# Signs written into half-words, weight bounds from Gram products, and a new order of work in a packed-attention and SoLU kernel

## The chip, the core and the metric

The kernel runs on one core of one Trainium2 chip. What counts is the device time of one execution, in microseconds; lower is better. Several executions were timed, and the median is given. The profile is of one execution more, and has its own time.

## What is computed

Eight batches of attention feed a two-layer network. First 32 learned rows `p` per head attend over 576 keys, and the result is used as both keys and values for the 576 queries. The output, 4608 tokens of 512 numbers, goes through a 512x1024 matrix, a softmax-weighted gate, a normalisation of each row and a 1024x512 matrix:

```python
p_packed = sm_attn(p, k, v)                    # 8 batches, 8 heads, 32x64
x = sm_attn(q, p_packed, p_packed)             # 576x64 for each head -> 4608 x 512
h = x @ w_in
e = np.exp(h - h.max(-1)); sm = e / (e.sum(-1) + 1e-09)
solu = h * sm
ln = (solu - mean) / np.sqrt(var + 1e-06) * g_ln
out = ln @ w_out                               # 4608 x 512
```

The two weight matrices arrive as float64. The kernel reads such a number as two 32-bit words and builds a float32 from them.

## The kernel before

**Stages.** All work is cut into named steps. `ORDER` (line 26 on) is a long string of step names; `perform` issues the steps in exactly that order, and `issue` chains all instructions of one engine in it. So each engine works through its own list, and a step that has to wait holds up whatever stands behind it on its engine. A letter behind a name picks the engine (`a` ScalarE, `v` VectorE, `p` GpSimd), a number the PSUM bank. Every load is issued from SyncE's queue (SP), in order too.

**Weights** (steps with `/w`, chunks 0 to 3 of `w_in`, 4 to 7 of `w_out`, 1 MB each). `lw`/`lW` loads a chunk into a buffer that later holds something else (`W_HOME`). `wa` (`exponents`) scales the upper words, `wl` (`last_bits`) shifts the lower words, `wm` (`magnitude`) joins the two, `wp` (`column_sums`) adds up the sizes on TensorE, and `ws` (`signed`) puts the sign in. `wb` (`bound_in`) and `pw` (`scale_out`) make powers of two from the sums. With these, `zw`, `zy` split `w_in`, and `ch`, `cl` split `w_out`, into pairs of f16 parts.

**Attention** (steps with `/b` for batch b). Keys, values and queries are loaded by `lk`, `lv`, `lq`. `s10`, `s11` are the first scores, `mx` their maxima (tile `nmx`), `ex` the exponentials, `tp` and `tc` their transposes, `av`, `pp`, `pt`, `pc` the packed rows, `un` the scale of the batch. `sx`, `sb`, `sm`, `su`, `se`, `ss`, `sn`, `at` are the second softmax; `ah`, `al` its f16 pair (tiles `a2h`, `a2l`). `z`, `zh`, `zl` multiply the packed rows by `w_in`, as an f16 pair.

**Token tiles** (steps with `-i`, 36 tiles of 128 rows). `m1` (line 642, 12 products of 512 columns, about 2.6 us) needs `a2` and `z` of its batch. Then come `nm`, `nb`, `bd`, `ex`, `u`, `mu`, `yd`, `yh`, `yl` on the other engines, `tr` (a DMA transpose), `m2a` and `m2b` (line 726, 24 products), `ev` and `st`, which stores the tile.

The scales that a step puts in place of a plain copy go through one helper, so line 139 or 141 in a profile stands for many steps, and the tile name tells which.

## Time and profile before

| | us |
|---|---|
| median of three runs | 392.41 (392.32 to 393.96) |
| time of the profiled execution | 392.76 |
| its span | 391.0 |
| TensorE busy in the span | 363.8 (93%) |
| VectorE busy | 297.0 (76%) |
| ScalarE busy | 229.3 (59%) |
| GpSimd busy | 193.7 (50%) |

The span is what the profile covers, from the first instruction to the end of the last store; the execution's own time is 1.76 us longer. Busy shares are means over the whole span. The first quarter and the rest of this kernel differ, so they are read by stretches below.

### The profile page before, as it was taken

Reading aid. Unit: us, or ns where it says so; the run is one execution under the profiler, and the core shown is the slowest. Engines: PE = TensorE matmul, PEld = TensorE weight load, DVE = VectorE, ACT = ScalarE, POOL = GpSimd, SP = SyncE. Lnnn points to the kernel's source line nnn. Section 1 sums busy time; section 2 is a strip of 40 time slices with the busy share of each in tenths; the row PEclk is TensorE's granted clock in tenths of the full one; section 3 lists DMA queues with packets and bytes.
Section 4 is the critical chain, followed back from the end, with each engine's and each line's share of the span. In section 5 each row is a group of like instructions: output and inputs, shape, how many; then the busy total and the mean of one; then the engine's idle time right before and its main releaser. Section 6 shows DMA issues by size and latency. Waiting matters only on the chain.

```text
span 391.0 us, 7708 instructions
## 1 busy us (share of the span) xinstructions
PE 363.8 (93%) x3056; PEld 168.3 (43%) x3056; DVE 297.0 (76%) x433; ACT 229.3 (59%) x367; POOL 193.7 (50%) x287
## 2 busy tenths in 40 slices
PE   5683879999999999999999999999999999999996
...
PEclk9575789999999999999999999999999999999999
...
GB/s 265 426 417 375 407 407 67 228 175 91 55 271 206 274 266 56 82 230 54 240 146 40 179 145 77 140 147 126 80 82 82 108 107 55 80 109 113 157 163 81
DMA packets 87957, 66.57 MB, mean 170 GB/s; under 512 B 76400, under 2 KB 76528, under 8 KB 86384
## 3 DMA queue, kind: packets, MB, share of 16 engines
...
## 4 chain that ended last, share of the span: by engine, by line
PE 67%; DVE 20%; DMA 4%; issue 3%; ACT 2%; POOL 1%; SPq 1%; DVEq 0%; ACTq 0%; POOLq 0%
PE pa L726 31%; PE ps L642 18%; PE ps L726 8%; DMA kT<-in_k_dram 3%; DVE u L671 3%; PE ps L534 2%; PE ps L476 2%; DVE nmx L400 2%; PE pa L442 2%; DVE zl L552 1%; DMA qT<-in_q_dram 1%; DVE ssum L411 1%; PE ps L396 1%; DVE wcl L296 1%; DVE e L202 1%
## 5 line engine op out<-in xcount | busy, mean ns | idle before, releaser
L726 PE MATMUL pa<-wch,yT 128*128 128x512 f16 x448 | 139.0, 380 | 0.3 <-DMA yT<-yhl 0.2
L726 PEld LDWEIGHTS <-yT 128*128 128x128 f16 x864 | 82.4, 98 | 105.8 <-issue 9.7
L726 PE MATMUL pa<-wcl,yT 128*128 128x512 f16 x224 | 84.9, 379 | 0.0
L671 DVE SCALAR_TENSOR_TENSOR u<-e,s_row,ps 128x1024 f32<-128x1024 f32 x36 | 45.9, 1275 | 19.0 <-ACT e L666 10.0
L648 DVE TENSOR_REDUCE nm<-ps 128x1 f32<-128x1024 f32 x36 | 43.7, 1218 | 19.2 <-PE ps L642 19.1
L642 PE MATMUL ps<-zh,a2h 128*128 128x512 f16 (+1 forms) x160 | 54.9, 381 | 0.7 <-DVE zl L552 0.4
L642 PE MATMUL ps<-zh,a2l 128*128 128x512 f16 (+1 forms) x160 | 54.6, 379 | 0.0
L642 PE MATMUL ps<-zl,a2h 128*128 128x512 f16 (+1 forms) x160 | 54.6, 379 | 0.0
L698 POOL TENSOR_TENSOR yhl<-u,yhl 128x1024 f16<-128x1024 f32 x16 | 35.3, 2206 | 37.8 <-ACT yhl L692 19.8
L666 ACT ACTIVATE e<-ps,bias,unit 128x1024 f32<-128x1024 f32 x36 | 43.3, 1203 | 9.1 <-DVE bias L141 8.4
L642 PEld LDWEIGHTS <-a2h 128*128 128x128 f16 (+1 forms) x320 | 27.7, 100 | 35.3 <-issue 5.2
L726 PE MATMUL ps<-wch,yT 128*128 128x512 f16 x128 | 39.9, 379 | 0.0
L659 POOL TENSOR_SCALAR bound<-nm,unit 128x1 f32<-128x1 f32 x20 | 10.9, 546 | 45.6 <-DVE nm L648 45.6
L682 ACT ACTIVATE u<-u,negmu 128x1024 f32<-128x1024 f32 x21 | 24.1, 1147 | 14.3 <-DVE negmu L141 9.5
L139 ACT ACTIVATE o_sb<-pa,c_row 128x512 f32<-128x512 f32 x16 | 11.0, 685 | 28.5 <-PE pa L726 16.1
L719 POOL TENSOR_TENSOR c_row<-c_row,neg_half 128x1 f32<-128x1 f32 x36 | 24.3, 674 | 3.0
L726 PE MATMUL ps<-wcl,yT 128*128 128x512 f16 x64 | 24.3, 379 | 0.0
L139 ACT ACTIVATE bias<-nm,unit 128x1 f32<-128x1 f32 x21 | 6.2, 295 | 30.0 <-DVE nm L648 29.8
L407 ACT ACTIVATE e<-ps,nmx 128x576 f32<-128x576 f32 x16 | 11.8, 736 | 19.6 <-DVE nmx L400 19.6
L700 DVE SCALAR_TENSOR_TENSOR yhl<-u,negmu,yhl 128x1024 f16<-128x1024 f32 x15 | 20.4, 1359 | 2.6 <-ACT yhl L694 2.5
L708 ACT ACTIVATE e<-u 128x1024 f32<-128x1024 f32 x21 | 22.1, 1051 | 0.1
L642 PEld LDWEIGHTS <-a2l 128*128 128x128 f16 (+1 forms) x160 | 14.3, 100 | 16.8 <-issue 0.2
...
## 6 DMA issues: line engine op xcount, KB each, us to landing
kT<-in_k_dram SPq DMA_DIRECT2D x16, 576.0 KB, 6.9
v<-in_v_dram SPq DMA_DIRECT2D x8, 1152.0 KB, 8.3
qT<-in_q_dram SPq DMA_DIRECT2D x16, 576.0 KB, 6.0
...
zl<-in_moe_w_in_dram SPq DMA_DIRECT2D x2, 1024.0 KB, 9.0
zh<-in_moe_w_in_dram SPq DMA_DIRECT2D x2, 1024.0 KB, 8.2
kT<-in_moe_w_out_dram SPq DMA_DIRECT2D x1, 1024.0 KB, 14.4
qT<-in_moe_w_out_dram SPq DMA_DIRECT2D x1, 1024.0 KB, 16.7
```

What stands on the lines that cost most here:

```text
L139: nc.scalar.activation(out, in_, AF.Copy, scale=scale)
L407: nc.scalar.activation(dst, src, AF.Exp, bias=st['nmx', r], accum_out=st['es'][:, r:r + 1])
L642: nc.tensor.matmul(h[rows, 512 * n:512 * n + 512], lhsT=lhsT, rhs=z[:, r, 512 * n:512 * n + 512], start=t == 0, stop=t == end)
L648: nc.vector.tensor_reduce(out=nm, in_=st['h'], axis=AX.X, op=ALU.max, negate=True)
L666: nc.scalar.activation(st['e'], st['h'], AF.Exp, bias=st['bias'], scale=st['unit'][:, 1:2], accum_out=st['se'])
L671: nc.vector.scalar_tensor_tensor(out=st['u'], in0=st['e'], scalar=st['s_row'], in1=st['h'], op0=ALU.mult, op1=ALU.mult, accum_out=st['su'])
L682: nc.scalar.activation(st['u'], st['u'], AF.Identity, bias=st['negmu'])
L698: engines[on(f'yl-{i}', 'v')].tensor_tensor(out=st['y'][:, 1], in0=st['u'], in1=st['y'][:, 0], op=ALU.subtract)
L700: nc.vector.scalar_tensor_tensor(out=st['y'][:, 1], in0=st['u'], scalar=st['negmu'], in1=st['y'][:, 0], op0=ALU.add, op1=ALU.subtract)
L708: nc.scalar.activation(st['e'], st['u'], AF.Square, bias=0.0 if centred() else st['negmu'], accum_out=st['sq'])
L719: nc.gpsimd.tensor_tensor(out=c_row, in0=c_row, in1=neg_half, op=ALU.pow)
L726: nc.tensor.matmul(st['po'], lhsT=st['yT'][:, a, c], rhs=w[:, c], start=c == 0 and t == 0, stop=c == NFC - 1 and t == 2)
```

## The change

**Sign.** A new step `wg` (`sign_bit`) writes each weight times 2^-60 as f16 into the upper half-words of the tile that holds the last bits. The product is too small for f16, so a zero with the weight's sign is left, and that is the sign bit of the word. `wl` now writes only the lower half-words of that tile. One step `wm` (`combined`) then joins exponent, last bits and sign on VectorE, where two did it; `ws` is gone. `wg` runs on ScalarE for chunks 0, 1 and 6 and on VectorE for 2, 3, 4, 5 and 7.

**Bounds.** `wp` (`squares`) now multiplies each 128-column piece of a chunk by itself on TensorE, eight products of 128 columns for a chunk where there were two of 512. `wb0`/`pw0` take the largest entry of each row on VectorE, `wb1`/`pw1` spread these over all partitions with a product, and `wb`/`pw` take the maximum again and an approximate root (`root`: a shift and an addition). The gain's bound comes from the sum of its squares (`gx`), and the GpSimd step `gm` is gone.

**Unread products.** `unread` issues four products of 512 columns whose result nobody reads. `ORDER` places four such steps: `hw5` and `hw11` among the loads of the weights, `hw13` and `hw2` behind the last `m2b` of the program.

**Places.** The whole string `ORDER` is new, with other engines for many steps. `unit` tiles have five buffers instead of four.

```diff
-lw1/w lw0/w wa1/w:a wl1/w:a wm1/w wa0/w:v wl0/w:a lp0/w wm0/w wp0/w:6 wp1/w lg/w ws1/w gx/w ws0/w lw2/w wa2/w:v pC0/w:p
...
+lW0/w wa4/w:p wl4/w wg4/w:v wm4/w lW1/w wa5/w:p wl5/w wp4/w:6 wg5/w:v wm5/w lW2/w wa6/w:a wl6/w wg6/w:a wm6/w wp5/w
...
     def last_bits(n):
-        last_of[n] = mlp.tile([P, DF], I32, name='u', bufs=2)
+        word = word_of(n)
         words = words_of(w_raw[n])[0]
...
-            nc.scalar.activation(last_of[n], words.bitcast(U32), AF.Copy, scale=LAST)
-
-    def magnitude(n):
-
-        bits = bits_of[n] = bits_of[n].bitcast(I32)
-        nc.vector.scalar_tensor_tensor(out=bits, in0=bits, scalar=3, in1=last_of[n], op0=ALU.logical_shift_left, op1=ALU.bitwise_or)
...
-    def column_sums(n):
-        m = n // 4
-        if n % 4 == 0:
-            sums[m] = one()
-        for i in range(2):
-            nc.tensor.matmul(sums[m], lhsT=g_abs[0][:, 2 * (n - 4) + i] if m else ones_b, rhs=upper(bits_of[n], i), start=n % 4 + i == 0, stop=n % 4 == 3 and i == 1)
-
-    def signed(n):
+            nc.scalar.activation(word.bitcast(U16)[:, 0::2], words.bitcast(U32), AF.Copy, scale=LAST)
+
+    def sign_bit(n):
+
+        scaled(on(f'wg{n}/w', 'a'), word_of(n).bitcast(F16)[:, 1::2], words_of(w_raw[n])[1].bitcast(F32), 2.0 ** (-60))
...
+    def combined(n):
+
...
-        nc.vector.scalar_tensor_tensor(out=dst.bitcast(I32), in0=words_of(w_raw[n])[1], scalar=-2147483648, in1=bits_of[n], op0=ALU.bitwise_and, op1=ALU.bitwise_or)
+        value[n] = dst
+        nc.vector.scalar_tensor_tensor(out=dst.bitcast(I32), in0=bits_of[n].bitcast(I32), scalar=3, in1=last_of[n], op0=ALU.logical_shift_left, op1=ALU.bitwise_or)
+
+    def squares(n):
+        m = n // 4
+        if n % 4 == 0:
+            sums[m] = one()
+        for i in range(NFC):
+            part = value[n].bitcast(BF16)[:, 2 * P * i + 1:2 * P * (i + 1):2]
+            nc.tensor.matmul(sums[m][:, :P], lhsT=part, rhs=part, start=n % 4 + i == 0, stop=n % 4 == 3 and i == NFC - 1)
+
+    def peaks(m):
+        peak_of[m] = small.tile([P, 1], F32, name=f'w_peak{m}')
+        nc.vector.tensor_reduce(out=peak_of[m], in_=sums[m][:, :P], axis=AX.X, op=ALU.max)
+
+    def spread(m):
+        nc.tensor.matmul(sums[m][:, P:2 * P], lhsT=peak_of[m].broadcast_to([P, P]), rhs=ident, start=True, stop=True)
...
+    def unread(dep):
+        spot = one()
+        for i in range(4):
+            ins = nc.tensor.matmul(spot, lhsT=ones_b, rhs=ones_b.unsqueeze(1).broadcast_to([P, 4, P]), start=True, stop=True)
...
```

**What moves, at three places.** SyncE's queue from its first load on, before (the name ahead of the arrow is the buffer; `in_moe_w_in` and `in_moe_w_out` are the weights, `in_k`, `in_v`, `in_q` the inputs of batch 0):

```order
L174 DMA zl<-in_moe_w_in_dram 128x2048
L174 DMA zh<-in_moe_w_in_dram 128x2048
L157 DMA pT<-in_p_dram 128x256
L164 DMA g_sb<-in_moe_g_ln_dram 128x8
L174 DMA zh<-in_moe_w_in_dram 128x2048
L378 DMA kT<-in_k_dram 128x1152 x2
L174 DMA zl<-in_moe_w_in_dram 128x2048
L382 DMA v<-in_v_dram 128x2304
L378 DMA qT<-in_q_dram 128x1152
L174 DMA kT<-in_moe_w_out_dram 128x2x1024
```

And the same queue from its first load on, after the change:

```order
L175 DMA kT<-in_moe_w_out_dram 128x2x1024
L175 DMA qT<-in_moe_w_out_dram 128x2x1024
L175 DMA v<-in_moe_w_out_dram 128x2x1024
L175 DMA zh<-in_moe_w_out_dram 128x2x1024
L165 DMA g_sb<-in_moe_g_ln_dram 128x8
L175 DMA zl<-in_moe_w_in_dram 128x2048
L175 DMA zh<-in_moe_w_in_dram 128x2048
L158 DMA pT<-in_p_dram 128x256
L410 DMA kT<-in_k_dram 128x1152 x2
L175 DMA zl<-in_moe_w_in_dram 128x2048
L414 DMA v<-in_v_dram 128x2304
L175 DMA zh<-in_moe_w_in_dram 128x2048
```

All four chunks of `w_out` now go ahead of the first keys, which three chunks of `w_in` went ahead of; two of `w_in` still do.

VectorE from the maxima of batch 0's first scores (`nmx`) on, before (`e`, `u` hold a chunk's exponents and last bits):

```order
L400 TENSOR_REDUCE nmx<-ps_76 128x1
L400 TENSOR_REDUCE nmx<-ps_77 128x1
L195 TENSOR_SCALAR u<-zh 128x1024
L202 SCALAR_TENSOR_TENSOR e<-e,u 128x1024
L411 TENSOR_SCALAR ssum<-es 128x2
L413 RECIPROCAL rs<-ssum 128x2
L219 SCALAR_TENSOR_TENSOR w_in_sb<-zh,e 128x1024
L202 SCALAR_TENSOR_TENSOR e<-e,u 128x1024
L219 SCALAR_TENSOR_TENSOR w_in_sb<-zl,e 128x1024
L453 TENSOR_REDUCE peak<-pp 128x1
```

And the same engine from the same two maxima on, after the change:

```order
L432 TENSOR_REDUCE nmx<-ps_76 128x1
L432 TENSOR_REDUCE nmx<-ps_77 128x1
L216 SCALAR_TENSOR_TENSOR w_in_sb<-e,u 128x1024
L327 SCALAR_TENSOR_TENSOR wcl<-yhl,gs,wch 128x512
L327 SCALAR_TENSOR_TENSOR wcl<-yT,gs,wch 128x512
L443 TENSOR_SCALAR ssum<-es 128x2
L445 RECIPROCAL rs<-ssum 128x2
L216 SCALAR_TENSOR_TENSOR w_in_sb<-e,u 128x1024
L327 SCALAR_TENSOR_TENSOR wcl<-yT,gs,wch 128x512
L148 COPY e1T<-ps_76 128x128
L327 SCALAR_TENSOR_TENSOR wcl<-yhl,gs,wch 128x512
```

Where a chunk cost two joins of 1024 columns there is one, and the low parts of `w_out` (`wcl`), which stood behind the start of the token tiles, fill the room.

TensorE up to the first products of token tile 3 (`a2h`, `zh`), before (`kT,pT` are first scores, `e` transposes of exponentials, `v,e1T` weighted values, `qT,ppT` second scores):

```order
L442 MATMUL pa_80<-v,e1T 32x64 x40
L458 MATMUL pa_79<-ident,pp 128x128 x2
L419 MATMUL pa_80<-ident,e_459 128x128 x4
L476 MATMUL ps_76<-qT,ppT 32x288 x8
L476 MATMUL ps_78<-qT,ppT 32x288 x8
L642 LDWEIGHTS a2h_101
L642 MATMUL ps_77<-zh,a2h_101 128x512
```

And the same stretch after the change:

```order
L474 MATMUL pa_79<-v,e1T 32x64 x40
L451 MATMUL pa_80<-ident,e_586 128x128 x4
L490 MATMUL pa_79<-ident,pp 128x128 x2
L451 MATMUL ps_77<-ident,e_586 128x128 x4
L508 MATMUL ps_78<-qT,ppT 32x288 x8
L456 MATMUL pa_80<-ident,e_586 64x64 x4
L508 MATMUL ps_76<-qT,ppT 32x288 x8
L428 MATMUL ps_77<-kT,pT 32x288 x8
L497 LDWEIGHTS ones_b
L497 MATMUL pa_79<-peak,ones_b 128x1
L428 MATMUL ps_78<-kT,pT 32x288 x8
L674 LDWEIGHTS a2h_101
```

The rest of batch 2's transposes, both halves of batch 3's first scores and one product on `peak` now stand ahead of tile 3.

## Rows read from the trace of the kernel before

**Rows 1.** The profile's page: span, engines, and three of its rows of 40 slices.

```profile
span 391.0 us, 7708 instructions
...
PE 363.8 (93%) x3056; PEld 168.3 (43%) x3056; DVE 297.0 (76%) x433; ACT 229.3 (59%) x367; POOL 193.7 (50%) x287
...
PE   5683879999999999999999999999999999999996
...
PEclk9575789999999999999999999999999999999999
...
GB/s 265 426 417 375 407 407 67 228 175 91 55 271 206 274 266 56 82 230 54 240 146 40 179 145 77 140 147 126 80 82 82 108 107 55 80 109 113 157 163 81
```

**Rows 2.** Busy time by stretches: PE, PEld, DVE, ACT, POOL; PEclk, DMA, GB/s.

```profile
55.00:100.00 45.00, 42.38 (x507) 20.47 (x507) 42.37 (x64) 34.48 (x64) 32.54 (x39) 1.00 0.49 153
100.00:380.00 280.00, 279.08 (x2088) 125.69 (x2083) 209.34 (x309) 161.65 (x253) 131.05 (x227) 1.00 0.51 134
```

**Rows 3.** TensorE in order of time: start, us, engine, line, operands, count.

```profile
13.72 2.53 PE L396 MATMUL ps<-kT,pT 64*32 64x288 f32 x32 [0.91 <-DMA kT<-in_k_dram]
...
54.75 0.50 PE L642 MATMUL ps<-zh,a2h 128*128 128x512 f16 x1
...
61.71 0.72 PE L396 MATMUL ps<-kT,pT 64*32 64x288 f32 x16
...
67.37 0.60 PE L419 MATMUL pa<-ident,e 128*128 128x128 f32 x4
...
386.70 0.38 PE L726 MATMUL pa<-wch,yT 128*128 128x512 f16 x1
```

**Rows 4.** The chain that ended last, in order of time, in its first 20 us.

```profile
3.77 11.23 DMA kT<-in_k_dram
```

**Rows 5.** VectorE in order of time, 0 to 55 us.

```profile
8.88 0.69 DVE L141 TENSOR_SCALAR e<-zh 128x1024 f32<-128x1024 f32 x1
9.67 1.23 DVE L202 SCALAR_TENSOR_TENSOR e<-e,u 128x1024 int32<-128x1024 int32 x1
...
17.75 2.13 DVE L202 SCALAR_TENSOR_TENSOR e<-e,u 128x1024 int32<-128x1024 int32 x1
...
25.79 0.15 DVE L242 TENSOR_SCALAR w_pow<-w_pow 128x1 f32<-128x1 f32 x1
...
26.93 0.78 DVE L498 STREAM_TRANSPOSE s<-ps 128x576 f32<-128x576 f32 x1
...
31.83 2.46 DVE L552 SCALAR_TENSOR_TENSOR zl<-ps,unit,zh 128x1024 f16<-128x1024 f32 x2
34.22 0.73 DVE L511 TENSOR_REDUCE sm<-s 128x18 f32<-128x576 f32 x1
...
48.51 1.41 DVE L400 TENSOR_REDUCE nmx<-ps 128x1 f32<-128x576 f32 x2
...
53.70 0.73 DVE L296 SCALAR_TENSOR_TENSOR wcl<-yhl,gs,wch 128x512 f16<-128x512 f32 x1
```

**Rows 6.** DMA issues: KB each, us from issue to landing.

```profile
kT<-in_k_dram SPq DMA_DIRECT2D x16, 576.0 KB, 6.9
v<-in_v_dram SPq DMA_DIRECT2D x8, 1152.0 KB, 8.3
...
zl<-in_moe_w_in_dram SPq DMA_DIRECT2D x2, 1024.0 KB, 9.0
...
pT<-in_p_dram SPq DMA_DIRECT2D x1, 128.0 KB, 8.0
```

**Rows 7.** GpSimd in order of time.

```profile
17.69 2.85 POOL L141 TENSOR_SCALAR e<-zl 128x1024 f32<-128x1024 f32 x1 [3.34 <-DMA zl<-in_moe_w_in_dram]
...
46.23 3.49 POOL L569 TENSOR_TENSOR a2l<-s,a2h 128x576 f16<-128x576 f32 x2 [0.41 <-ACT a2h L145]
```

**Rows 8.** ScalarE in order of time.

```profile
6.60 1.10 ACT L197 ACTIVATE u<-zl 128x1024 int32<-128x1024 uint32 x1
...
46.20 0.68 ACT L145 CAST a2h<-s 128x576 f16<-128x576 f32 x1
```

More of the change, by code (lines that the diff above doesn't have):

```diff
@@ L12 @@
 U32 = mybir.dt.uint32
+U16 = mybir.dt.uint16
 AF = mybir.ActivationFunctionType
@@ new lines @@
+wp6/w hw5/w:7 lW3/w wa7/w:a wl7/w wg7/w:v wm7/w wp7/w lg/w hw11/w:7 pw0/w lw1/w wa1/w:a lw0/w wa0/w:p gx/w pw1/w lp0/w
+pC0/w:a pw/w ch6/w:v lk0/0 lk1/0 wl1/w wg1/w:a s10/0:0 wl0/w s11/0:2 mx0/0 mx1/0 ch4/w:p lw3/w lv/0 wm1/w cl6/w ex0/0
+ex1/0 cl4/w rs/0 tp0/0:7 tp1/0:6 tp2/0:0 wg0/w:a wm0/w ch0/w:p ch5/w:a cl0/w tc0/0:a tc1/0:a tc2/0:v av/0:7 ch7/w:a
+cl7/w wp0/w:6 wa3/w:v wl3/w wg3/w:v wp1/w lw2/w wa2/w:a wl2/w wg2/w:v ch2/w:a wm3/w pp/0:a pt/0:7 lq0/0 pc/0:a lp1/w
+sx0/0:4 cl2/w pe/0 wm2/w wp2/w sb0/0 sm0/0 wp3/w wb0/w pC1/w:a lk0/1 su0/0:p s10/1:2 mx0/1 ex0/1 lk1/1 s11/1:0 mx1/1
@@ L90 @@
+sq-35 m2a-34:6 ca-33 cr-34 m2b-34 ca-28 mu-33:p cr-28 ex-31 u-31 yd-33:a yh-33:a yl-33:p ev-28:v tr-35 m2a-35:7 m2b-35
+mu-31:v yd-31:a tr-33 m2a-33:0 m2b-33 sq-33 ev-34:v yh-31:a yl-31:v st-34 st-28 tr-31 m2a-31:6 ca-31 cr-33 cr-35 ev-35:v
+m2b-31 st-35 ev-33:a st-33 sq-31 cr-31 hw13/w:7 hw2/w:7 ev-31:a zz/7 st-31
 '''
@@ L304, in unit_of @@
     def unit_of(b, total):
-        unit = units[b] = small.tile([P, 6], F32, name='unit', bufs=4)
+        unit = units[b] = small.tile([P, 6], F32, name='unit', bufs=5)
         power_of(unit[:, 5:6], total, unit[:, 4:5])
@@ L357, in issue @@
         fn(*args)
+        made[now[0]] = nc.cur_bb.bb.instructions[-1].name
         for ins in nc.cur_bb.bb.instructions[n:]:
@@ L763, in preparation @@
         at('gx', gain_sizes, after=['lg'])
-        at('gm', gains, after=['gx'])
         for n in range(8):
```

178 lines of the change are left out of this document (95 added, 83 removed).

## The prediction

> **What bounds the kernel now.** I read the page first, then the busy time by stretches, then TensorE and VectorE in order of time. On the page TensorE is busy for 93% of the span, but its slices show two kernels: a start of six slices, some 55 us, with holes and a clock far below full, and a rest that is full [rows 1]. The stretches say it more sharply. From 100 to 380 us TensorE is busy for 279.08 of 280 us at full clock, from 55 to 100 us for 42.38 of 45 us, while VectorE has room in the rest (209 of 280 us) [rows 2]. So the reader can take the kernel as a queue of TensorE work that begins with the first product of token tile 3, at 54.75 us, and ends with the last product at 386.70 + 0.38 = 387.08 us [rows 3]. Between them lie 332.3 us, of which 2.6 + 0.9 = 3.5 us are idle, so 328.8 us of work. Call the beginning F. The time can change by F, by what is done ahead of F, and by those 3.5 us. Joins saved on VectorE are worth nothing by themselves after 100 us.
>
> What sets F? Before it VectorE hardly stops: the chain of its operations runs from the landing of batch 0's keys at 3.77 + 11.23 = 15.0 us [rows 4] to the maxima of batch 2's first scores, whose end is 48.51 + 1.41 = 49.9 us [rows 5], and F follows 4.9 us later. The loads are the other limit: over the first six slices they move 265 to 426 GB/s [rows 1], so bytes in front of the keys are time.
>
> **The change, part by part.**
>
> *Loads.* Before, three weight chunks, a piece of `p` and the keys come to 3 x 1.05 + 0.13 + 2 x 0.59 = 4.46 MB by 15.0 us [rows 4, 6]. A slice is 9.775 us; the slices give 2.59 MB by 9.8 us and 4.81 MB by 15.0 us [rows 1], so 0.35 MB of later loads are then already moved. After it, six chunks go ahead: 7.60 + 0.35 = 7.95 MB. The slices reach 6.75 MB at 19.55 us and go on at 417 GB/s, so the keys land at 22.4 us, 7.4 us later than before. That is a loss, and the VectorE work that filled those 7.4 us must be gone for it to be paid back.
>
> *VectorE.* The `w_out` joins lie ahead of the keys now, where VectorE waits for loads anyway (2 us of each 2.5 us chunk: one join of 1.23, one sign of 0.69 [rows 5]), so I cost them at nothing; the late loads hide them. What is left from the keys to batch 2's maxima, counted from the new order: 4 joins at 1.23 (4.9), 3 scalings or signs at 0.69 (2.1), 6 low parts `wcl` at 0.73 (4.4), 6 maxima at 0.70 (4.2), 3 transposes at 0.78 (2.3), 3 reductions over 576 at 0.73 (2.2), one `zl` at 1.23, and 19 short ones at 0.15 plus some 0.05 between them (3.8) [rows 5]: 25.1 us. Before, this stretch took 34.9 us, with eleven joins in it. A sign written with a step of two half-words stands in no row. Its bounds are 0.69, the scaling of float32 with a step, and 1.23, the join; I take 0.69, being the same kind of operation, and 1.23 would add 1.1 us for the two signs here.
>
> *Slowed operations.* The join at 17.75 took 2.13 us where the one at 9.67 took 1.23 [rows 5]; a GpSimd scaling ran from 17.69 to 20.54 us beside it [rows 7]. Four of those eleven joins were slowed so, by 0.8 to 1.0 us. GpSimd has less to do in the new stretch (one `e` and one `w_hi` scaling less), so I count one slowed operation, 0.9 us; both ends are in the rivals. The Trainium skill, "SBUF — State Buffer", Terms, says that VectorE and GpSimd share a port pair under an exclusive lock held for the whole instruction, and that the loser fully blocks. Here the rows differ from it: the join began 0.06 us after the GpSimd scaling and ended at 19.88 us, 0.66 us ahead of it. By the rows the sum gets 0.9 us; by the rule it would get up to 2.85 us.
>
> *F.* VectorE starts on the list at about 23 us and ends at 23 + 25.1 + 0.9 = 49.0 us. Behind it stand a sum of three operations (1.1), two short ones (0.3), `zl` (1.2) and a transpose (0.8), to 52.4 us [rows 5], then ScalarE's `a2h` at 0.68 [rows 8] and GpSimd's `a2l` at 1.75 [rows 7]: F = 54.9, say 55.0 us. The later keys and the shorter list cancel.
>
> *ScalarE* gains three signs of about 1.10 us [rows 8], with slack: they stand by the loads. *TensorE*: the squares, eight products of 128 columns for two of 512, and the eight spare products of `hw5`, `hw11` lie where it waits for chunks; without that cover the spare ones would cost 3.4 us at half clock. `hw13` and `hw2` stand behind the last product, beside the last store; the end has 391.0 - 387.1 = 3.9 us for that, and they take 8 x 0.21 = 1.7 us.
>
> *Work moved ahead of F.* Both halves of batch 3's first scores (0.65 each: the 0.72 is followed 0.64 us later by the next work), the rest of batch 2's transposes (0.44 + 0.38) and a peak product (0.1): 2.2 us [rows 3]. They are in TensorE's holes there, so they leave the queue for good.
>
> *Idle after F.* Of the 3.5 us, most lies between 55 and 100 us, where VectorE is busy for 42.37 of 45 us [rows 2]. Seven `wcl` stood there before, two do now: 5 x 0.73 = 3.7 us less in front of the maxima and gates that TensorE waits for. Against it, 2.2 us of cover are gone that TensorE had while tile 3 was on its way to `m2a`. The ends are 0 and 3.7; I take 1.5 us.
>
> **The sum.** 55.0 + 328.8 - 2.2 + 1.5 = 383.1 us for the last product, + 3.9 = 387.0 us span against 391.0. The profiled execution took 1.76 us more than its span, so 388.8 against its 392.76; the median lies 0.35 below that execution: **388.4 us** against 392.41. A measurement here can tell about 0.5%, 1.96 us, from no change, so this is faster if it falls under 390.4.
>
> **Rivals.**
>
> 1. *The list runs clean* (faster still). No operation is slowed (0.9 less), and no idle is left after F (1.5 less); the loads keep 426 GB/s, the best slice [rows 1], which brings the keys 0.3 us earlier. 388.4 - 2.7 = 385.7. For it: less GpSimd work. Against: four of eleven were slowed before.
>
> 2. *GpSimd slows as before* (no change). 13 operations of the list are joins, `wcl`, scalings or signs. At four in eleven, 4.7 of them lose 0.9, 4.2 in all: 3.3 more than I count, F = 58.3, and 391.7. The signs at 1.23 alone would give 389.5. For it: `wch` and `w_hi` scalings of GpSimd still lie in the stretch. By the lock as a mechanism, the same 4.7 operations would wait 2.85 each: 13.4 - 0.9 = 12.5 more, and 400.9. The Trainium skill, "SBUF — State Buffer", Terms, is the page for it. The trace speaks against it, as above, so it gets 2 in 100.
>
> 3. *The loads become the bound of F* (slower). Batch 3's keys must now land ahead of tile 3, because its first scores stand there in TensorE's queue. All that is loaded ahead of them and they come to 18.9 MB, 19.25 with what runs ahead; the slices reach 18.47 MB at 48.9 us and 19.25 at 50.8 us [rows 1]. First scores of 1.3 us then end at 52.1, 2.9 us ahead of F. These keys need a buffer that the scores of batch 1 give back. If TensorE comes to those late (they stand behind the squares of the last `w_in` chunk), SP's queue stops, and with it every load behind. From F = 59 on, with the keys landing near 57.7, the gain of 4.0 us is gone; at F = 61.5 it is 394.9. For it: 7 us that the change has already spent. Against it: 17.8 MB of earlier loads stand ahead of these keys, and by 40 us the slices have moved 14.9 MB, so scores that come by then leave the queue 8 us of loads to go on with.
>
> 4. *The start gets shorter by the clock.* The granted clock is 5 to 8 tenths in the slices between 10 and 58 us [rows 1], that is, part of the time at 1.2 GHz. The new products lie at 10 to 21 us and not in the holes behind, so I give it no gain of its own; where VectorE sets F it would have none.
>
> **Chances.** Forecast 0.50, its own range 386.6 to 390.4; clean list 0.20; GpSimd as before 0.18; lock 0.02; loads 0.10. Faster by over 0.5%: forecast and clean list, 0.70 less 0.02 for the forecast's edge = 0.68. Within 0.5%: GpSimd as before 0.18, that edge 0.02, and 0.02 of the loads = 0.22. Slower: the other 0.08 of the loads and the lock = 0.10. The range takes in the clean list and GpSimd as before, with their edges: 385.0 to 392.4.
>
> **What the profile will show.** Keys of batch 0 landing near 22.4 us; batch 2's maxima ending near 49; signs on VectorE at 0.69; the first product of tile 3 at 55 with batch 3's first scores ahead of it; idle of TensorE after it near 1.5 us; full clock from there on. I am wrong if F differs by more than 3 us, or if the full queue behind it shows holes of several us that it had not before, as in front of the first `m2a`.

## The result, and the profile after

The changed kernel takes 387.83 us (median of four runs, 387.67 to 388.0) against 392.37 us (median of four) of the kernel before beside it: a ratio of 0.988, 95% interval 0.9848 to 0.9911. I had forecast 388.4 us. The profiled execution took 387.9 us and its span is 386.1 us, against 392.76 and 391.0.

The page of the changed kernel, its span, engines and two of the rows of slices that [rows 1] shows of before:

```profile
span 386.1 us, 7861 instructions
...
PE 366.6 (95%) x3126; PEld 172.9 (45%) x3126; DVE 284.3 (74%) x453; ACT 231.1 (60%) x370; POOL 184.9 (48%) x273
...
PE   4578799999999999999999999999999999999997
...
PEclk9565999999999999999999999999999999999999
```

And its busy time by stretches, which answers to [rows 2]:

```profile
55.00:100.00 45.00, 44.70 (x493) 21.43 (x493) 42.01 (x70) 33.77 (x59) 32.69 (x42) 1.00 0.66 193
100.00:380.00 280.00, 279.93 (x2097) 125.46 (x2096) 202.88 (x310) 157.12 (x254) 127.75 (x210) 1.00 0.50 131
```

The start is no shorter; the queue behind it has become full. TensorE's idle between 55 and 380 us is 0.30 + 0.07 = 0.37 us, where it was 3.5 us. TensorE in order of time shows where the queue begins and ends, to be read against [rows 3]:

```profile
21.96 1.28 PE L428 MATMUL ps<-kT,pT 64*32 64x288 f32 x32
...
54.24 0.69 PE L428 MATMUL ps<-kT,pT 64*32 64x288 f32 x16
...
54.97 0.71 PE L428 MATMUL ps<-kT,pT 64*32 64x288 f32 x16
55.62 0.39 PE L674 MATMUL ps<-zh,a2h 128*128 128x512 f16 x1
...
381.50 0.38 PE L758 MATMUL pa<-wch,yT 128*128 128x512 f16 x1
381.72 1.89 PE L260 MATMUL pa<-ones_b 128*128 128x512 bf16 x8
```

F is 55.62 us, 0.87 later than before. From F to the end of the last product that is read, 381.50 + 0.38 = 381.88 us, it is 326.3 us, where it was 332.3. Of those 6.0 us 3.1 us are idle that is gone. Counted by its products, the work that now stands ahead of F is 2.2 us: 32 first scores of batch 3 (1.3), at 54.24 and 54.97, 12 transposes (0.8) and one product on `peak` (0.1). The other 0.7 us has no row of its own; the profile models the ends of products, so short holes in the kernel before may hide in it, which is not shown. The eight unread products at the end lie beside the last stores; from the last product that is read to the end of the span it is 4.2 us, where it was 3.9. Together +0.9 - 6.0 + 0.3 = -4.8, and the spans differ by 4.9 us.

The prediction had named VectorE's list as what sets F. VectorE in order of time, signs (`u`), joins (`yT`, `yhl` for `w_out`, `w_in_sb` for `w_in`) and the ends of the list, to be read against [rows 5]:

```profile
5.57 0.75 DVE L142 TENSOR_SCALAR u<-kT 128x1024 f16<-128x1024 f32 x1 [4.25 <-DMA kT<-in_moe_w_out_dram]
9.02 2.12 DVE L216 SCALAR_TENSOR_TENSOR yT<-e,u 128x1024 int32<-128x1024 int32 x1 [2.70 <-POOL e L142]
...
24.20 1.42 DVE L432 TENSOR_REDUCE nmx<-ps 128x1 f32<-128x576 f32 x2
25.53 1.21 DVE L216 SCALAR_TENSOR_TENSOR w_in_sb<-e,u 128x1024 int32<-128x1024 int32 x1
26.66 1.18 DVE L327 SCALAR_TENSOR_TENSOR wcl<-yhl,gs,wch 128x512 f16<-128x512 f32 x1
...
49.62 0.74 DVE L432 TENSOR_REDUCE nmx<-ps 128x1 f32<-128x576 f32 x1
```

From the maxima of batch 0 to those of batch 2 it is 24.20 to 49.62 + 0.74 = 50.4 us, 26.2 us; I had counted 25.1 + 0.9 = 26.0, from 23 us. Its size came out right, in part by luck: 1.7 us of it are four waits, which the sum did not have, and the operations with the gaps between them come to 24.5 us. That the list is the bound was not right, as the chain that ended last already hints. In this part of it (start, us, what), nothing of VectorE stands for 15 us, from 24.98 to 39.70:

```profile
24.98 1.55 ACT e L439 x4
26.54 1.26 ACT u L140
27.80 0.56 ACT wch L140
...
31.04 1.16 ACT e L140
32.20 1.26 ACT u L198
33.46 0.56 ACT wch L140
34.02 0.52 ACT pp L140 x2
34.58 0.70 PE pa L490 x2
35.31 0.38 ACT ppT L146
35.73 1.22 PE ps L508 x16
36.95 1.82 PE pa L224 x16
38.77 0.90 PE ps L428 x16
39.70 1.42 DVE nmx L432 x2
```

From batch 0's exponentials on it is ScalarE's own queue: a sign, a high part of `w_out`, last bits, exponents, another high part, and behind all of these batch 0's probabilities (`pp`), for which TensorE waits. The load of the last chunk of `w_in` is as late as that queue: issued at 17.05 us, it lands 13.7 us later, 0.3 us ahead of the exponents at 31.04 us that read it. From 34.58 to 39.70 us most of the chain is TensorE's own work, at a granted clock of 0.58 from 34.5 to 40 us. ScalarE in order of time gives the lengths, for 1024 columns each: a sign into half-words, last bits into half-words, exponents into whole words.

```profile
26.43 1.37 ACT L140 ACTIVATE u<-zh 128x1024 f16<-128x1024 f32 x1
...
29.83 1.35 ACT L198 ACTIVATE u<-zl 128x1024 uint16<-128x1024 uint32 x1
31.04 1.16 ACT L140 ACTIVATE e<-zh 128x1024 f32<-128x1024 f32 x1
```

I had put both writes at the 1.10 us of [rows 8].

### The profile page after: what moved, and what is told of

Its sections match the earlier page's. It is cut to its first block, busy times and chain, and to the rows that moved or that the text cites. A ratio compares the mean times of both kernels' runs of the same rounds, so it can differ in the third digit from the quotient of the medians.

```text
span 386.1 us, 7861 instructions
## 1 busy us (share of the span) xinstructions
PE 366.6 (95%) x3126; PEld 172.9 (45%) x3126; DVE 284.3 (74%) x453; ACT 231.1 (60%) x370; POOL 184.9 (48%) x273
## 4 chain that ended last, share of the span: by engine, by line
PE 86%; ACT 5%; DVE 3%; DMA 3%; POOL 1%; issue 1%; POOLq 0%
PE pa L758 38%; PE ps L674 24%; PE ps L758 10%; PE ps L566 3%; PE ps L508 3%; PE ps L428 2%; PE pa L474 2%; DMA yT<-yhl 1%; PE pa L260 1%; DMA kT<-in_moe_w_out_dram 1%; PE pa L224 1%; POOL e L142 1%; DVE yT L216 1%; ACT e L439 1%; ACT u L198 1%
## 5 line engine op out<-in xcount | busy, mean ns | idle before, releaser
L758 PE MATMUL pa<-wch,yT 128*128 128x512 f16 x464 | 144.1, 379 | 0.1
L758 PE MATMUL pa<-wcl,yT 128*128 128x512 f16 x232 | 87.9, 379 | 0.0
L714 ACT ACTIVATE u<-u,negmu 128x1024 f32<-128x1024 f32 x23 | 26.2, 1145 | 23.2 <-POOL negmu L142 12.7
L758 PE MATMUL ps<-wch,yT 128*128 128x512 f16 x112 | 34.8, 379 | 0.0
L744 POOL TENSOR_SCALAR s_eps<-se,s_row 128x1 f32<-128x1 f32 x36 | 15.9, 443 | 37.5 <-DVE s_row L693 20.7
L750 POOL TENSOR_SCALAR c_row<-sq,k_out,s_eps 128x1 f32<-128x1 f32 x36 | 13.6, 378 | 30.9 <-ACT e L740 27.9
L740 ACT ACTIVATE e<-u 128x1024 f32<-128x1024 f32 x23 | 24.2, 1051 | 0.1
L751 POOL TENSOR_TENSOR c_row<-c_row,neg_half 128x1 f32<-128x1 f32 x36 | 21.9, 608 | 3.0
L548 POOL TENSOR_TENSOR s<-s,sm 128x1152 f32<-128x1152 f32 (+1 forms) x6 | 10.8, 1805 | 21.7 <-DVE negmu L142 9.2
L758 PE MATMUL ps<-wcl,yT 128*128 128x512 f16 x56 | 21.2, 379 | 0.0
L530 DVE STREAM_TRANSPOSE s<-ps 128x576 f32<-128x576 f32 x16 | 12.5, 783 | 11.6 <-PE ps L508 11.2
L536 POOL TENSOR_TENSOR s<-s,mx 128x1152 f32<-128x1152 f32 (+1 forms) x8 | 15.1, 1887 | 10.6 <-DVE mx L533 10.5
```

The lines of the kernel that those rows point to most:

```text
L536: by('su', x).tensor_tensor(out=part(st['w'], x), in0=part(st['w'], x), in1=spread(st['mx'], x), op=ALU.subtract)
L714: nc.scalar.activation(st['u'], st['u'], AF.Identity, bias=st['negmu'])
L740: nc.scalar.activation(st['e'], st['u'], AF.Square, bias=0.0 if centred() else st['negmu'], accum_out=st['sq'])
L744: nc.gpsimd.tensor_scalar(out=s_eps, in0=st['se'], scalar1=1e-09, scalar2=st['s_row'], op0=ALU.add, op1=ALU.mult)
L750: nc.gpsimd.tensor_scalar(out=c_row, in0=st['sq'], scalar1=k_out[:, 0:1], scalar2=s_eps, op0=ALU.mult, op1=ALU.add)
L751: nc.gpsimd.tensor_tensor(out=c_row, in0=c_row, in1=neg_half, op=ALU.pow)
```

## The experiments

The theory that I went in with: VectorE's list sets F, and the gain is work moved ahead of F and idle gone behind it. The rivals: loads or the clock set F; the low parts or the moved scores were hidden anyway; ScalarE. In the table F is the start of tile 3's first product, and "behind F" the time from there to the end of the last product that is read, both from each kernel's profiled execution, which need not be a median one (391.48 us for the first new order, whose median is 393.14). The ratio is to the kernel before, with its 95% interval. Line numbers stand one higher in some kernels, where `ORDER` has a row more or the code a line.

| kernel | median us | ratio | F | behind F |
|---|---|---|---|---|
| before | 392.4 | 1 | 54.75 | 332.3 |
| changed | 387.83 | 0.9880 [0.9848, 0.9911] | 55.62 | 326.3 |
| no unread products | 387.63 | 0.9866 [0.9846, 0.9887] | 55.66 | 326.8 |
| scores of batch 3 behind F | 391.18 | 0.9972 [0.9955, 0.9988] | 53.96 | 330.8 |
| `w_in` joins twice | 392.58 | 1.0005 [0.9993, 1.0018] | 60.10 | 326.8 |
| `w_out` joins twice | 390.19 | 0.9936 [0.9916, 0.9955] | 57.54 | 327.0 |
| five low parts behind F | 393.46 | 1.0030 [1.0012, 1.0048] | 55.90 | 331.4 |
| early exponents on ScalarE | 387.66 | 0.9877 [0.9852, 0.9902] | 54.96 | 326.0 |
| all signs on VectorE | 388.27 | 0.9896 [0.9878, 0.9914] | 55.22 | 326.3 |
| first new order | 393.14 | 1.0015 [0.9998, 1.0032] | 59.24 | 326.3 |
| probabilities earlier | 388.65 | 0.9893 [0.9875, 0.9910] | 54.96 | 326.6 |
| half-words twice | 392.54 | 0.9999 [0.9986, 1.0012] | 60.66 | 326.1 |
| all joins twice | 396.01 | 1.0086 [1.0072, 1.0099] | 63.01 | 326.7 |
| ScalarE relieved | 387.26 | 0.9857 [0.9837, 0.9877] | 55.84 | 326.4 |

The last column is the table's main finding: the changed kernels fall into two groups. It is 326.0 to 327.0 us for every kernel with the new order behind F, and 330.8 and 331.4 us for the two that put a part of the old order back. The column F is less sharp. By 50 us one execution lay 1.4 us ahead of another in the same order, where the granted clock differed (see "Scores of batch 3 behind F"); a difference in F below that says little.

**No unread products.** All four steps are taken out of `ORDER`; two of them stand here.

```diff
-... wp5/w wp6/w hw5/w:7 lW3/w ... lg/w hw11/w:7 pw0/w ...
+... wp5/w wp6/w lW3/w ... lg/w pw0/w ...
```

> The changed kernel without its four steps of unread products (hw5, hw11, hw13, hw2); all else in the same order. My prediction costed them at nothing, hidden by the loads: 387.8 us within 0.4, the first product of tile 3 (F) still at 55.6. Rival, the chain: in the changed kernel hw5 and hw11 run from 16.9 to 21.4 us, between the squares of the last w_out chunk and the product that spreads their peaks, and the maxima of batch 0 wait behind that on VectorE from about 22.7 to 24.2; then taking them out brings those maxima 1.4 us forward, F by 0.5 to 1.4, and the time to 386.4 to 387.3. Rival, the clock: the unread products keep TensorE's clock up; then the granted clock between 20 and 55 us falls below 0.50 to 0.67 and 1.00 as it is now, and the time rises by 1 us or more.

Measured: 387.63 us and F 55.66 us, both as in the changed kernel. The keys are waited for now (a wait of 0.66 us ends the idle time before batch 0's first scores). The first of batch 0's maxima begins 0.9 us earlier, at 23.26 us, and nothing of that arrives: the probabilities are behind the last chunk of `w_in`, which lands at 31.0 us, and batch 1's maxima begin at 39.73 us, where they began at 39.70. The unread products cost nothing where they stand, and buy nothing that can be measured.

**Scores of batch 3 behind F.** Batch 3's first scores, maxima and exponentials go behind tile 3's row maxima, and batch 2's `av` with them.

```diff
-... s10/3:2 mx0/3 ex0/3 al1/0:p pk/1 s11/3:4 mx1/3 ch1/w:a ex1/3 un/1 m1-3:0 nm-3 ... av/2:7 ...
+... al1/0:p pk/1 ch1/w:a un/1 m1-3:0 nm-3 s10/3:2 mx0/3 ex0/3 s11/3:4 mx1/3 ex1/3 av/2:7 ...
```

> The changed kernel with batch 3's first scores (s10, s11, with their maxima and exponentials) put back behind the first products of token tile 3, and batch 2's weighted values with them, so that tile 0 still has its bank. My prediction: these 1.3 us of products fill holes ahead of F; put back, they lengthen the queue behind F by 1.3 us while F stays within 0.3 of 55.6: 389.1 us. Rival: in the changed kernel TensorE is full from 51.3 us to F, so the scores push F back by what they take; put behind it, F falls by 1.3 to 54.3 and the time stays at 387.8 within 0.4.

Measured: F is 1.7 us earlier, and the time 391.18 us. The earlier F is mostly not the edit's doing. TensorE in order of time, at batch 0's second scores and the squares behind them, at batch 2's first transposes, and at F:

```profile
35.64 0.72 PE L509 MATMUL ps<-qT,ppT 64*32 64x288 f32 x16 [0.46 <-ACT ppT L147]
36.41 1.09 PE L225 MATMUL pa<-w_in_sb 128*128 128x128 bf16 x16
...
49.05 0.33 PE L452 MATMUL pa<-ident,e 128*128 128x128 f32 x1 [0.38 <-ACT e L440]
...
53.96 0.38 PE L675 MATMUL ps<-zh,a2h 128*128 128x512 f16 x1 [0.83 <-DVE s L531]
```

Every engine's list is that of the changed kernel up to batch 3's scores, and the transposes stand ahead of them. Still they begin at 49.05 us, and in the changed kernel at 50.49. The 1.4 us arise where TensorE's products stand on the chain: from 34.5 to 40 us the granted clock is 0.97 here and 0.58 there, and the same second scores took 0.72 and 1.22 us. From the transposes to F it is 4.91 us, against 5.13 with the scores in between. TensorE now waits 0.83 us for VectorE just ahead of F, so the scores lay in a hole but for some 0.2 us, as forecast. And the time rose. TensorE's stretches show why (columns as in [rows 2]):

```profile
65.00:70.00 5.00, 3.11 (x53) 1.81 (x55) 4.97 (x8) 4.89 (x10) 2.49 (x2) 0.90 0.00 0
70.00:75.00 5.00, 5.00 (x86) 2.68 (x75) 4.59 (x9) 4.52 (x8) 3.28 (x4) 0.76 0.82 108
```

Batch 3's softmax now runs when TensorE has nothing to do but wait for it: 1.9 us of idle between 65 and 70 us, and behind the hole the granted clock falls to 0.90 and 0.76 in the two stretches (in windows of 1 us it is 0.50 from 69 to 72 us and 1.00 from 73 on). At 1.00 they would have held some (0.10 + 0.24) x 5 = 1.7 us more work, an estimate from these rows. The queue is 4.5 us longer than in the changed kernel: 1.7 us more idle (2.07 against 0.37), 1.3 us of scores back in it, and 1.5 us left, about what the estimate gives.

**Joins twice.** The joins of four chunks are issued twice, with the same result.

```diff
+        for again in range(2 if n < 4 else 1):
             nc.vector.scalar_tensor_tensor(out=dst.bitcast(I32), in0=bits_of[n].bitcast(I32), scalar=3, in1=last_of[n], ...)
```

First those of `w_in`:

> The changed kernel with the joining operation of chunks 0 to 3 (w_in) issued twice, writing the same values: 4 more operations of 1.2 us in VectorE's list between batch 0's keys and F, as many as the saved joins of these chunks. My prediction, VectorE's list sets F: F moves by 4 x 1.15 = 4.6, less the 1.7 us for which VectorE is idle in the list, so 2.9 to 4.6, and the time is 390.7 to 392.4. Rival, the loads and ScalarE set F and VectorE has room: F moves by less than 1.5 and the time is under 389.3.

Then, with `n >= 4`, those of `w_out`:

> The changed kernel with the joining operation of chunks 4 to 7 (w_out) issued twice, writing the same values: 4 more operations of 1.2 us on VectorE ahead of batch 0's keys. My prediction: loads hide them, VectorE is idle for 10 of its first 20 us there; 387.8 us within 0.5. Rival, joins saved are worth their time wherever they stand: 4.6 us, 392.4. Between the two, if the chain of chunk 7 through squares, peaks and the scale of w_out holds the maxima of batch 0 up: one join of 1.2 us, 389.0.

Measured: four `w_in` joins, 4 x 1.21 = 4.8 us more on VectorE, move F by 4.5 us and the time by 4.75 us. Four `w_out` joins, which I had costed at nothing, move F by 1.9 us and the time by 2.4 us. The squares and unread products on TensorE and the scale of `w_out` on VectorE follow those joins, and batch 0's maxima stand behind the scale. They begin at 27.26 us, 3.1 us later, and batch 1's at 41.60, 1.9 us later. So the late loads hide half of such a join and not all of it.

**Five low parts behind F.** `cl` of chunks 2, 0, 6, 5 and 7 goes behind tile 3's first products, so that one stands ahead of it and not six.

```diff
-... pw/w ch6/w:v ... wm1/w cl6/w ... ch5/w:a cl0/w ... cl7/w ... cl2/w pe/0 ... at0/0 cl5/w ...
+... nm-3 ... nb-3:v cl2/w cl3/w ... rs/3 cl0/w nm-0 cl6/w ... mu-3:v cl5/w ... mu-0:p cl7/w ...
```

> Five low parts of w_out (chunks 0, 2, 5, 6, 7) go back behind the first products, so that one stands ahead of tile 3 instead of six; all else stays. Theory (VectorE's list sets F): the list loses 5 x 0.74 = 3.7 us, or 4.1 us if the slowed one of 1.18 us is among them, and F falls from 55.6 to between 51.5 and 53; the same 3.7 us then stand in front of tile 3's maxima and gates, so idle of TensorE behind F goes from 0.4 to some 2.5 us and the 2.2 us of moved scores and transposes lose part of their cover: 386.5 to 388.5 us, about the time of the changed kernel. If my term for them was right (they were the cause of idle of 2 us behind F), the time falls by 1 to 2 us less than F does. Rival A: the low parts lie in holes of VectorE, F stays at 55.6 and the time rises by up to 3.7 us, to 391. Rival B: they were worth nothing behind F either: F falls by 3.7 us and so does the time, to 384.

Measured: rival A by F, and dearer than any of the three had it. The list lost 5 low parts (3.7 us, and the slowed one among them), F stayed at 55.90 us, and the time rose by 5.6 us to more than that of the kernel before. VectorE's time ahead of F went into holes; one of them, and the chain from the same load on:

```profile
31.36 0.78 DVE L143 TENSOR_SCALAR u<-zh 128x1024 f16<-128x1024 f32 x1 [0.81 <-DMA zh<-in_moe_w_in_dram]
...
34.89 0.29 DVE L486 TENSOR_REDUCE peak<-pp 128x1 bf16<-128x128 f32 x1 [1.66 <-ACT pp L141]
```

```profile
17.18 14.09 DMA zh<-in_moe_w_in_dram
...
31.37 1.18 ACT e L141
32.55 1.24 ACT u L199
33.79 0.57 ACT wch L141
34.35 0.52 ACT pp L141 x2
...
34.91 0.61 PE pa L491 x2
```

The last chunk of `w_in` lands at 31.27 us, ScalarE needs 3.0 us for it and a high part, and only then come the probabilities that TensorE waits for. So with a shorter list the bound is a load and ScalarE's queue behind it. The same load stands in the chain of five more kernels, where it lands between 30.6 and 31.1 us: no unread products, scores of batch 3 behind F, early exponents on ScalarE, first new order, probabilities earlier. Behind F the five low parts stand in the way. TensorE by stretches:

```profile
65.00:70.00 5.00, 3.44 (x35) 1.34 (x33) 4.93 (x9) 4.54 (x9) 1.84 (x1) 0.92 0.49 206
70.00:75.00 5.00, 5.00 (x100) 3.25 (x93) 4.96 (x7) 1.85 (x4) 1.87 (x4) 0.74 0.79 63
75.00:80.00 5.00, 3.44 (x30) 1.28 (x28) 4.93 (x9) 3.96 (x9) 3.65 (x2) 1.00 0.20 45
```

VectorE is busy for 4.93 of 5 us and more throughout, TensorE has 3.1 us of holes here and 0.4 us in the ten before, and the clock falls behind one of them as above, which by the same estimate costs (0.08 + 0.26) x 5 = 1.7 us of work.

**Early exponents on ScalarE.** GpSimd's two scalings at the start go to ScalarE.

```diff
-lW0/w wa4/w:p wl4/w ... lW1/w wa5/w:p ...
+lW0/w wa4/w:a wl4/w ... lW1/w wa5/w:a ...
```

> The exponents of the first two w_out chunks are scaled by ScalarE (about 1.1 us each) instead of GpSimd (2.82 us each). Theory: beside GpSimd's scaling the join at 9.02 took 2.12 instead of 1.21 us and the sign at 11.06 took 1.34 instead of 0.75; both go back to their lengths, 1.5 us of VectorE work less ahead of the keys, and about half of what lies there reaches F (as the doubled w_out joins showed): F 54.9 to 55.6, 387.0 to 387.8 us. Rival A (GpSimd takes the port from VectorE for a whole instruction, and the early chain is held up by that): more than 1.5 us come back, F under 54.5, 386 or less. Rival B: ScalarE becomes late with the half-words, joins come later, F over 56, 388.5 or more.

Measured: 387.66 us, no change in the time; F is 0.66 us earlier, within the clock's share. The lengths did what was expected. The same join beside no GpSimd scaling:

```profile
8.05 1.23 DVE L217 SCALAR_TENSOR_TENSOR yT<-e,u 128x1024 int32<-128x1024 int32 x1 [1.67 <-ACT u L199]
```

It took 2.12 us beside one (from 8.97 to 11.79 us, the join from 9.02 to 11.14). So GpSimd's scaling was the cause of the 0.9 us. The join ended 0.65 us ahead of GpSimd's instruction, as far as the profile's rough spans on GpSimd go, so it was not held up until the end of it. Another operation was: the sum `ssum` at 44.73 us took 0.50 us in the changed kernel, where its like took 0.16 us, and ended at 45.23 us, beside a GpSimd scaling from 42.35 to 45.19 us. And the join at 25.53 us took its full-speed 1.21 us beside two GpSimd scalings (23.86 to 28.17 us). The Trainium skill, "SBUF — State Buffer", Terms, has the loser of the shared port fully blocked; `ssum` agrees with that, and the two joins do not. What tells them apart was not tried.

**All signs on VectorE.** The three signs of ScalarE go to VectorE.

```diff
-... wg6/w:a ... wg1/w:a ... wg0/w:a ...
+... wg6/w:v ... wg1/w:v ... wg0/w:v ...
```

> The three signs that ScalarE writes (chunks 6, 1, 0: 1.33 to 1.37 us each) go to VectorE (0.74 us each), so ScalarE writes no sign at all. Theory: the sign of chunk 0 at 26.4 us falls into VectorE's list and adds 0.74 us there; the other two stand ahead of the keys where half of the added work reached F before, so 0.7 us at most: F 56.3 to 57.1, 388.4 to 389.2 us. Rival A: ScalarE's signs, 4 us in all, stand in front of the exponents that VectorE waits for; without them the joins come earlier and F falls below 55.3, 387.3 or less. Rival B: nothing moves, 387.8, F within 0.3 of 55.6.

Measured: 388.27 us and F 55.22 us. No case fits both numbers: F fell by 0.4 us, which is within the clock's share, though VectorE's list got longer, and the time can't be told from that of the changed kernel. Which of the two engines writes these three signs is worth nothing measurable here.

**First new order.** Meant to be faster. The unread products go, `su1/0` and `se1/0` go ahead, `cl5` goes back, and batch 1's first scores go ahead of `wm2`, `wp2`, `wp3`, `wb0`. I described `wm2` as squares; it is the join of the last chunk.

```diff
-... cl2/w pe/0 wm2/w wp2/w sb0/0 sm0/0 wp3/w wb0/w pC1/w:a ... s10/1:2 mx0/1 ... s11/1:0 mx1/1 ...
+... cl2/w pe/0 sb0/0 sm0/0 pC1/w:a ... s10/1:2 mx0/1 ... s11/1:0 wm2/w wp2/w wp3/w wb0/w mx1/1 ...
```

> A version meant to be faster: the unread products are left out, batch 1's first scores stand ahead of the squares of the last two w_in chunks, GpSimd subtracts the second half of the second maxima ahead of the scaling by the sums of the first half, ScalarE's second exponentials stand ahead of its high parts accordingly, and the low part of chunk 5 goes behind batch 2's second maxima. No operation is added or removed but the unread products. Theory: idle of VectorE in the list (0.60 us in front of batch 1's maxima) and ScalarE's wait of 1.05 us at 48 us are gone, so batch 2's exponentials come 1 to 1.3 us earlier; F 54.0 to 55.0, idle behind it still under 1 us: 386.2 to 387.3 us. Rival A: the squares that now come later hold up the scale of w_in, whose ten short operations follow them on VectorE; F stays at 55.6 and the time at 387.8. Rival B: the list is all that counts, its sum is unchanged, 387.6 as without the unread products.

Measured: rival A's mechanism, several times its price: F 59.24 us, 393.14 us. VectorE in order of time, at the join and at the peaks of the squares that follow it:

```profile
39.03 1.62 DVE L217 SCALAR_TENSOR_TENSOR w_in_sb<-e,u 128x1024 int32<-128x1024 int32 x1
41.84 0.29 DVE L229 TENSOR_REDUCE w_peak<-pa 128x1 f32<-128x128 f32 x1 [1.19 <-PE pa L225]
```

The join stood at 35.21 us before the move. It now waits behind a maximum that waits for the scores, and with it the squares, the scale of `w_in` and everything in `z`. The 3.8 us of the join come back as 3.6 us of F in the profiled execution. That one took 391.48 us, the fastest of twelve; the other 1.7 us of the median are in no trace.

**Half-words twice.** ScalarE writes the last bits of the four `w_in` chunks twice.

```diff
+            for again in range(2 if n < 4 else 1):
                 nc.scalar.activation(word.bitcast(U16)[:, 0::2], words.bitcast(U32), AF.Copy, scale=LAST)
```

> ScalarE writes the last bits of the four w_in chunks into the half-words twice (4 x 1.35 us more on ScalarE, nothing else changed). Theory (ScalarE's queue is as long as VectorE's list between 25 and 36 us): of the four, the first two stand at 20 to 23.7 us with 1.25 us of idle behind them, the other two at 29.8 to 33.4 us without any; at least the latter reach F: 2.7 to 4 us, F 58.3 to 59.6, 390.5 to 392 us. Rival (ScalarE has slack here, as my prediction had it): F within 0.7 us of 55.6, 387.5 to 388.5 us.

Measured: F 60.66 us, 5.04 us later, and 392.54 us, for 4 x 1.25 = 5.0 us more on ScalarE (one write follows the next by 1.25 us). That is more than the theory had. ScalarE in order of time, at batch 0's exponentials and probabilities:

```profile
26.65 0.71 ACT L440 ACTIVATE e<-ps,nmx 128x576 f32<-128x576 f32 x1
...
38.34 0.60 ACT L140 ACTIVATE pp<-pa,rs 128x128 f32<-128x128 f32 x2
```

The exponentials of batch 0 begin 1.7 us later than in the changed kernel (24.98), so the idle of 1.25 us that stood ahead of them took up 0.8 of the first two writes. The probabilities come 4.4 us later (33.91), and the last 0.6 us are added behind them. From batch 0's exponentials on, ScalarE had no slack.

**All joins twice.** All eight, so that VectorE has as many joins as before.

> All eight joins are issued twice, so that VectorE has as many joins as the two-step join of before had, in the new order. Theory (the two parts add up, 4.8 us for w_in and 2.4 us for w_out): F 62 to 63, 394 to 395.5 us, slower than the kernel before: the new order without the shorter join would lose. Rival A: the two overlap, since both wait for the same loads: F 60, 392.5 to 393 us. Rival B: the slower start gives cover back behind F, so that the time rises by under 4 us, under 392.

Measured: F 63.01 us, 396.01 us. The two parts add up: 7.4 us of F, where 4.5 and 1.9 gave 6.4; 8.2 us of time, where 4.75 and 2.4 gave 7.1. The queue behind F stays at 326.7 us. So with as many joins as the kernel before, the new order is slower than it.

**Probabilities earlier.** Without the unread products; `pp/0`, `pt/0` ahead of the last chunk's half-words; batch 1's scores and maxima ahead of the last squares, and behind the last join.

```diff
-... wp1/w lw2/w wa2/w:a wl2/w wg2/w:v ch2/w:a wm3/w pp/0:a pt/0:7 lq0/0 pc/0:a lp1/w sx0/0:4 cl2/w pe/0 wm2/w wp2/w ...
+... lw2/w wa2/w:a pp/0:a pt/0:7 wl2/w wg2/w:v wm3/w wp1/w lq0/0 pc/0:a ch2/w:a lp1/w sx0/0:4 cl2/w pe/0 pC1/w:a lk0/1 wm2/w ...
```

> After five low parts less in VectorE's list left F where it was, the chain there ran from a late chunk of w_in through ScalarE's queue: the probabilities of batch 0 (0.61 us) stand behind that chunk's exponents, half-words and a high part. This version leaves out the unread products, puts batch 0's probabilities and their transposes ahead of the chunk's half-words, and batch 1's first scores and maxima ahead of the last squares (not ahead of the last join). Theory (ScalarE's queue and VectorE's list are of one length there, so both must get shorter): batch 1's maxima begin at 37.8 to 38.5 instead of 39.70 us, 1.4 us of VectorE's idle are filled, F 54.0 to 55.0, idle behind F 0.4 to 1.0: 386.3 to 387.3 us. Rival A: the squares are late by 0.8 us, the scale of w_in with them, the high and low parts of z follow it: F 55.6 or later, 387.6 to 388.5. Rival B: F falls as the theory says and the whole of it comes back as idle behind F, 387.6.

**ScalarE relieved.** The same, with `ch7`, `ch2` on GpSimd and `wa4`, `wa5` on ScalarE.

```diff
-lW0/w wa4/w:p ... lW1/w wa5/w:p ... ch7/w:a ... ch2/w:a ...
+lW0/w wa4/w:a ... lW1/w wa5/w:a ... ch7/w:p ch2/w:p ...
```

> The order with batch 0's probabilities ahead of the late half-words, plus relief for ScalarE: the high parts of w_out chunks 7 and 2 (0.70 us each on ScalarE) go to GpSimd (2.15 us each), which has 10.5 us of idle from 28.2 us on, and the exponents of the first two w_out chunks go from GpSimd to ScalarE, ahead of the keys. Theory (ScalarE's queue from 25 to 36 us sets F microsecond for microsecond, as the doubled half-words showed): 1.4 us less there, F 53.2 to 54.3, idle behind F 0.4 to 1.0, 386.0 to 387.0 us. Rival A: GpSimd beside VectorE slows one or two of its joins by 0.9 us each; F 54.5 to 56, 387 to 388.5 us. Rival B: what F gains comes back as idle behind it: F under 54.3 and still 387.5 us or more.

Measured: 388.65 and 387.26 us, F 54.96 and 55.84. Neither can be told from the changed kernel. The scores came early, as meant; VectorE in order of time in the second of them:

```profile
37.76 0.76 DVE L433 TENSOR_REDUCE nmx<-ps 128x1 f32<-128x576 f32 x1 [0.38 <-PE ps L429]
...
40.37 0.29 DVE L229 TENSOR_REDUCE w_peak<-pa 128x1 f32<-128x128 f32 x1 [0.83 <-PE pa L225]
```

Batch 1's maxima begin 1.9 us earlier (39.70 before), but the largest entries of the squares come 1.6 us later (38.81 before), and the scale of `w_in` with them. Loads stand ahead of both. ScalarE in order of time, in the same kernel:

```profile
31.27 1.18 ACT L141 ACTIVATE e<-zh 128x1024 f32<-128x1024 f32 x1 [1.60 <-DMA zh<-in_moe_w_in_dram]
```

The time taken from ScalarE's queue has become a wait of 1.60 us for the last chunk of `w_in`. The rest of `p` lands at 34.69 us, and batch 1's scores, and the squares behind them in TensorE's queue, wait for its scaling. So the bound is no longer the softmax, but these loads and the squares. None of my versions beats the changed kernel by more than the intervals allow.

## Why the prediction was right, and where it was not

**The time** came out 0.6 us below the forecast and the span 0.9 us, by a sum with errors of opposite sign: F 0.6 us later than I had it, the queue behind F 1.8 us shorter (326.3 for 328.1), the tail 0.3 us longer. How near F came is in part luck, with 1.4 us of clock between executions and the terms below.

**Loads.** The keys of batch 0 were to land at 22.4 us. With the unread products the first half isn't waited for at 21.96 us, and without them a wait for a key load ends at 21.75 us (in the kernel with early exponents, one for the second half at 22.75), so this held within a microsecond. The loss was paid back as forecast: F moved by 0.87 us, less than the clock's share, and not by seven.

**VectorE's list.** Its length was right (26.2 for 26.0 us), but by 1.7 us of waits in place of work. Its start was 24.2 and not 23 us, since eight short operations on the scale of `w_out` and a high part stand ahead of it. These follow the `w_out` joins: "I cost them at nothing; the late loads hide them" was half wrong, as those joins issued twice showed. From the end of the list to F it was 5.3 us and not 6.0, by another path: not through VectorE's sum, `zl` and `a2l`, but through batch 2's exponentials and TensorE, which is busy for 4.30 of the 4.33 us from 51.29 us to F.

**What sets F.** This is the step that failed. I had VectorE's list as the bound and "*ScalarE* gains three signs of about 1.10 us, with slack". Added work showed VectorE on the path (4.5 us of F for 4.8 us of joins), but work taken from it moved nothing (five low parts less: F +0.3 us). On ScalarE 5.0 us more moved F by 5.04 us. And with ScalarE relieved it waited 1.60 us for the last chunk of `w_in`. So three run level, VectorE's list, ScalarE's queue and that load, with the squares' chain close behind: more work on either engine lengthens F at nearly its full price, and less work on one alone does not shorten it by a price. ScalarE's price was low too: a write into half-words took 1.33 to 1.37 us, not 1.10. That this made the 0.6 us by which F is late is not shown: without any sign on ScalarE F was 0.4 us earlier.

**Signs on VectorE** took 0.74 to 0.76 us; the end that I took was 0.69, the other 1.23.

**Slowed operations.** I counted one in the list, 0.9 us. There were two, 0.8 us in all: `wcl` at 26.66 us took 1.18 us and not 0.74, and `ssum` at 44.73 us 0.50 and not 0.16, both beside GpSimd scalings. The rivals that had none, or four, fell. When I read from the join at 17.75 us of the kernel before that VectorE is not held until GpSimd's end, I left out the `ssum` behind it: at 19.80 us it took 0.76 us and ended with GpSimd's scaling.

**Moved work.** I had 2.2 us leaving the queue, and by the count of products it was 2.2. "They are in TensorE's holes there" held but for some 0.2 us: with batch 3's scores behind F, F comes 4.91 us after batch 2's first transposes, and with them ahead of it 5.13. What I left out is that behind F they cost a hole besides their 1.3 us of queue.

**Idle behind F** was the mis-sized term: 0.4 us and not 1.5. The ends that I gave were 0 and 3.7. What went wrong in it is that I let the two causes work against each other (fewer low parts, less cover); the runs show both at work in the same direction: low parts back behind F lengthen the queue by 5.1 us, the scores back by 4.5, and the whole gain in the queue is 6.0. Either edit undone gives back most of it, so they don't add up, and it seems that each needs the other; both undone together were not tried. The clock that falls behind a hole, 1.5 to 1.7 us of these prices, was in no term of mine.

**The rivals.** Batch 3's keys did not become the bound: TensorE goes from the work ahead of them to batch 3's scores at 54.24 us without a wait. Another load runs level with the bound, that of the last chunk of `w_in`, which the third rival did not name. The unread products gave no gain by the clock: without them it was 0.50 and not 0.80 from 20 to 25 us, and the time was the same. "Where VectorE sets F it would have none" did not hold for the start as a whole: from 34.5 to 40 us TensorE's own products are on the chain, and the clock there was worth 1.4 us of F.

**Open:** Why the granted clock from 34.5 to 40 us is 0.58 in one execution and 0.97 in another of the same order, and what F would be with VectorE's list, ScalarE's queue and the load shortened together, was not tried.
